# A spectral-plus-dense layer on one core: fewer opening fills on TensorE, and three GpSimd steps set further back

## The chip, the cores and the metric

The kernel runs on one core of a Trainium2 chip. TensorE (PE in the profile) does the matmuls, VectorE (DVE), ScalarE (ACT) and GpSimd (POOL) do the elementwise work, and SyncE (SP) issues the DMA transfers. The metric is device time in microseconds (us), the median over several runs.

## The reference, cut to what matters

Two stages over one tensor x of 2048 rows by 512 columns in bf16:

```python
h  = x + irfft2(rfft2(layernorm(x)) * (w_r + 1j * w_i))
h2 = h + relu(layernorm(h) @ w1 + b1) ** 2 @ w2 + b2
```

The layernorms run along the 512 columns. The kernel does the Fourier transforms as matmuls with tables of sines.

## The kernel before, in words

**Tiling.** The 2048 rows lie on 128 partitions, 16 rows ("groups", g = 0 to 15) on each, so a tile of one group is 128x512. The opening does three things at once: it loads x in six DMA pieces, it takes mean and variance of each group (`bn_stats` on DVE, line 385, with two groups on ACT, lines 376 and 379), and it builds the tables of sines from index tiles.

**Tables.** GpSimd writes index tiles with `iota` (line 293). DVE, ACT or GpSimd multiply them into phases (`fiE` at lines 340 and 342, `fiG` at line 332, `fiI` at line 461), and ACT takes the sine. `KF` (line 335, DVE) is a mask table: for each partition it keeps the values of `kft` where a comparison holds, zero elsewhere. `idxE` has 1152 elements a partition, and line 342 (GpSimd) is the wide operation on it; line 340 is its twin on ACT.

**First transform step.** For each group g, the mask table is scaled by the reciprocal deviation of the rows: `rs` is raised to the power -0.5 on GpSimd (line 392) in batches of 2, 4, 4, 3, 2 and 1 groups, and `KR[g] = KF * rs` (line 401: groups 0 to 8 on GpSimd, 10 to 15 on DVE; group 9 on ACT, line 398). Four matmuls a group (lines 408 and 409, function `s1`) then use `KR[g]`. Groups 0 to 9 go in five pairs into wide PSUM tiles (`m_p`, two buffers), each emptied into `Bt` by one ACT copy (line 424). Groups 10 to 15 go in units into narrow PSUM tiles (`s_p`, four buffers), emptied by ACT and DVE in turn (line 440). The next step (line 505) reads all of `Bt`, and after it a chain of DVE, ACT and PE work runs through the spectrum to about 48 us, followed by the two dense matmuls (lines 905 and 934) to the end.

**Fills.** At the very start TensorE has nothing to do. `fill` (line 356) issues matmuls of a zero tile `fz` against itself, 128x512 each, so that TensorE is running when the first real matmul comes. There are eight such calls, planned 0.9 us apart. Besides, every new PSUM tile calls `warm` (line 234), which adds small 128x128 matmuls of zeros where the plan sees a gap of over 0.3 us on TensorE:

```python
for _ in range(min(20, int(plan.gap * 0.6 / 0.0625)) if plan.gap > 0.3 else 0):
    mm(p[:, 0:P], lhsT=fz[:, 0:P], rhs=fz[:, 0:P], start=True, stop=True)
```

**What sets the order.** All steps are handed to a planner (class `Plan`) with an engine, an estimated duration, what they read and write, a priority (lower goes first) and an optional `order` (start after the named step). It plays the program through once with these estimates and issues the instructions in the order found; the order on each engine is then fixed by `pin`. What the planner takes as `reads` or `order` only shapes this order. The waits that the chip makes come from the data that an instruction really touches. So a step that is listed as reading `KF`, but does not touch it, gets a place in the queue from that and no wait.

**Other names.** `ident` is the 128x128 identity (lines 311 and 312), read by TensorE first at line 471 (at 28.9 us) and then for residuals and transposes. `idxD` is the index tile that `fiI` (line 461) is made from; `GI`, its sine, is taken on ACT at 34.5 us. `pF[:, 5:7]` (line 459, DVE copy of two integers a partition, from the `iota` of line 309) is the multiplier for `fiI`.

Of the kernel before, what the change touches and what calls it, by code (L numbers as in the profile page):

```python
# [9 lines left out]
ALU = mybir.AluOpType  # L10
# [5 lines left out]
P = 128  # L16
QT = 16384
# [16 lines left out]
class Plan:  # L34
# [13 lines left out]
    def add(self, eng, w, fn, reads=(), writes=(), prio=0.0, alloc=None, at=0.0, shared=False, lag=0.0,  # L48
            uses=(), order=()):
        many = isinstance(eng, tuple)  # L50
        ways = dict(zip(eng, w)) if many else {eng: w}
        t = dict(many=many, eng=None, ways=ways, w=0.0, fn=fn, reads=list(reads), writes=list(writes), prio=prio, alloc=alloc, at=at,
                 shared=shared, lag=lag, end=None, order=list(order), n=len(self.tasks))
        self.tasks.append(t)
        for k in t["writes"]:
            self.made.setdefault(k, []).append(t)
        for k in set(t["reads"]) | set(t["writes"]) | set(uses):
            self.use.setdefault(k, []).append(t)
# [82 lines left out]
def kernel(  # L141
# [17 lines left out]
    G = 16  # L159
# [16 lines left out]
    ident = persist.tile([P, P], BF16, name="ident")  # L176
# [19 lines left out]
    KF = fwd.tile([P, 2, P], BF16, name="KF")  # L196
    KR = fwd.tile([P, G, 2, P], BF16, name="KR")
# [10 lines left out]
    pI = tab.tile([P, 8], I32, name="pI")  # L208
    pF = tab.tile([P, 8], FP32, name="pF")
    cE = tab.tile([P, 1], FP32, name="cE")  # L210
# [4 lines left out]
    idxE = tab.tile([P, 9 * P], I32, name="idxE")  # L215
# [3 lines left out]
    fiE = [tab.tile([P, 9 * P], I32, name=f"fiE{i}") for i in range(2)]  # L219
    fiI = tab.tile([P, 4, 256], I32, name="fiI")  # L220
    idxD = tab.tile([P, 256], I32, name="idxD")
# [4 lines left out]
    gp, ve, sc, pe, sy = nc.gpsimd, nc.vector, nc.scalar, nc.tensor, nc.sync  # L226
# [5 lines left out]
    add = plan.add  # L232
# [31 lines left out]
    for c, (a, b) in enumerate(CH):  # L264
        add("SP", 0.45, lambda a=a, b=b: sy.dma_start(xs[:, a:b, :], xv[:, a:b, :]),
            writes=[("x", g) for g in range(a, b)], prio=c, at=0.7, lag=LAND[c])
# [4 lines left out]
    for i in range(2):  # L271
        add("SP", 2.0, lambda i=i: sy.dma_start(wx[i][:].rearrange("k j l -> j k l"),
                                                wv[i].rearrange("k j l -> j k l")[9:16, ::-1, 1:L + 1]),
            writes=[("wx", i)], prio=6 + i, at=1.0, lag=5.0)
    for i in range(2):
        add("SP", 1.0, lambda i=i: (sy.dma_start(W[:, i], wv[i][:, 0:8, 1:L + 1]),
                                        sy.dma_start(W[:, 2 + i, 0], wv[i][:, 8, 1:L + 1])), writes=[("Wn", i)],
            prio=8 + i, at=1.0, lag=6.0)
    for i in range(2):
        add("SP", 1.0, lambda i=i: sy.dma_start(W[:, 2 + i, 1:8], wx[i][:, ::-1]), reads=[("wx", i)], writes=[("Wr", i)],  # L280
            prio=10 + i, lag=6.0)

    def pool(w, fn, prio, reads=(), writes=()):
        add("POOL", w, fn, reads=reads, writes=writes, prio=prio)

    def dve(w, fn, prio, reads=(), writes=(), shared=False, **k):
        add("DVE", w, fn, reads=reads, writes=writes, prio=prio, shared=shared, **k)
# [4 lines left out]
    def iota(dst, pattern, base, cm):  # L292
        gp.iota(dst, pattern=pattern, base=base, channel_multiplier=cm)
# [4 lines left out]
         writes=["idxE"])  # L298
    pool(0.14, lambda: iota(pI[:, 3:5], [[16384, 2]], 0, 128), 0.15, writes=["p1"])
    pool(0.2, lambda: iota(rowq[:].rearrange("p h (k u) -> p h k u", u=2), [[0, 2], [4096, 8], [0, 2]], 0, 0), 0.4,  # L300
         writes=["rowq0"])
    pool(0.1, lambda: gp.memset(rowq[:, :, 1:2], 8 * 4096), 0.5, reads=["rowq0"], writes=["rowq"])
    pool(0.2, lambda: iota(offq[:].rearrange("p h (k u) -> p h k u", u=2), [[-HT, 2], [0, 8], [-QT, 2]], QT, 0), 0.6,
         writes=["offq0"])
# [3 lines left out]
         writes=["idxG"])  # L308
    pool(0.14, lambda: iota(pI[:, 5:7], [[128, 2]], 128, 256), 1.0, writes=["p2"])
    pool(0.1, lambda: gp.memset(mhalf[:], -0.5), 0.85, writes=["mhalf"])  # L310
    pool(0.1, lambda: gp.memset(ident[:], 0.0), 1.2, writes=["id0"])
    pool(0.3, lambda: gp.affine_select(out=ident[:], in_=ident[:], compare_op=ALU.not_equal, fill=1.0, base=0,
                                       pattern=[[-1, P]], channel_multiplier=1), 1.3, reads=["id0"], writes=["ident"])
    pool(0.34, lambda: iota(idxD[:], [[1, 256]], 0, 0), 1.4, writes=["idxD"])

    dve(0.15, lambda: ve.memset(mv1[:], 0.0), 0.06, writes=["mv1z"])
    dve(0.15, lambda: ve.memset(qtc[:], float(QT)), 0.0, writes=["qtc"])
# [3 lines left out]
        reads=["p0"], writes=["p01"])  # L321
    dve(0.15, lambda: ve.tensor_single_scalar(pI[:, 2:3], pI[:, 0:1], 7, ALU.bitwise_and), 0.2,
        reads=["p0"], writes=["p02"])
    dve(0.15, lambda: ve.scalar_tensor_tensor(cE[:], pI[:, 1:2], -4064.0, pI[:, 7:8], ALU.mult, ALU.add), 0.3,
        reads=["p01", "p7"], writes=["cE"], shared=True)
    dve(0.17, lambda: ve.tensor_copy(pF[:, 0:5], pI[:, 0:5]), 0.4, reads=["p01", "p02", "p1"], writes=["pF"],
        shared=True)
    dve(0.2, lambda: ve.scalar_tensor_tensor(flat(fiK), flat(rowq[:]), pF[:, 1:2], flat(offq[:]), ALU.mult, ALU.add),
        0.4, reads=["pF", "rowq", "offq"], writes=["fiK"], shared=True)
    for t in range(2):  # L330
        for r in range(2):
            add(("DVE", "POOL")[t], (0.36, 0.46)[t], lambda t=t, r=r: (ve, gp)[t].tensor_scalar(
                fiG[:, t, r, :], idxG[:], pF[:, 3 + t:4 + t], float((QT, HT)[r]), ALU.mult, ALU.add),
                prio=(0.45, 0.92)[t], reads=["pF", "idxG"], writes=[("fiG", t)])
# [4 lines left out]
    dve(0.3, lambda: ve.memset(fz[:], 0.0), 0.05, writes=["fz"])  # L339
    act(1.26, lambda: sc.activation(fiE[0][:], idxE[:], ACT.Identity, scale=cE[:]), 0.3, reads=["idxE", "cE"],  # L340
        writes=["fiE0"])
    pool(1.4, lambda: gp.tensor_scalar(fiE[1][:], idxE[:], cE[:], float(QT), ALU.mult, ALU.add), 0.95,
         reads=["idxE", "cE"], writes=["fiE1"])
    act(0.2, lambda: sin_of(flat(kft[:]), lo(fiK[:])), -50.0, reads=["fiK"], writes=["kft"])
    for t in range(2):
        act(0.62, lambda t=t: sin_of(flat(GF[:, t]), lo(flat(fiG[:, t]))), 0.6 + t / 10, reads=[("fiG", t)],
            writes=[("gf", t)])
    dve(0.15, lambda: ve.tensor_scalar(GF[:, :, :, 255:256], GF[:, :, :, 255:256], 0.5, None, ALU.mult), 54.0, reads=[("gf", 0), ("gf", 1)],
        order=[("KR", G - 1)], writes=["GF"])
    for i in range(2):  # L350
        act(1.16, lambda i=i: sin_of(flat(EF[:, i]), lo(fiE[i][:])), 0.5 + i / 10, reads=[f"fiE{i}"],
            writes=[f"EF{i}"])
    dve(0.46, lambda: ve.tensor_scalar(EF[:, 2], EF[:, 0], -1.0, None, ALU.mult), 78.0, reads=["EF0"],
        order=["BtD"], writes=["EF2"])

    def fill(key, n, prio, reads=(), at=0.0):
        def go():
            p = sg_tile(key)
            for _ in range(n):
                mm(p[:, 0:512], lhsT=fz[:, 0:P], rhs=fz[:], start=True, stop=True)  # L360
        add("PE", n * 0.216, go, reads=["fz", *reads], writes=[key], prio=prio, alloc=("sg", key), at=at)

    for i in range(8):
        fill(("fa", i), 4 if i < 6 else 3, -1.0, at=1.3 + 0.9 * i)

    ON_ACT = (3, 6)
    SQ = 5
# [4 lines left out]
    for bi, (a, b) in enumerate(BATCH):  # L372
        z = 10 * min(bi, 4) + 10
        for g in range(a, b):
            if g in ON_ACT:
                act(0.76, lambda g=g: sc.activation(junk[:], xs[:, g, :], ACT.Identity, scale=-RT / D,
                                                    accum_out=nmr[:, g:g + 1]), z - 30, reads=[("x", g)],
                    writes=[("sm", g)])
                act(0.82, lambda g=g: sc.activation(junk[:], xs[:, g, :], ACT.Square, scale=RT, bias=nmr[:, g:g + 1],
                                                    accum_out=mv1[:, g, 1:2]), z - 30, reads=[("x", g), ("sm", g), "mv1z"],  # L380
                    writes=[("mv", g)])
            else:
                def bn(g=g):
# [4 lines left out]
                    writes=[("mv", g)])  # L388
        mvs = [("mv", g) for g in range(a, b)]
        dve(0.13, lambda a=a, b=b: ve.tensor_scalar(rs1[:, a:b], mv1[:, a:b, 1], EPS, float(WSC ** -2), ALU.add, ALU.mult), z - 1,  # L390
            reads=mvs, writes=[("va", bi)])
        pool(0.42 + 0.155 * (b - a), lambda a=a, b=b: gp.tensor_tensor(rs1[:, a:b], rs1[:, a:b], mhalf[:, 0:b - a],
                                                                     ALU.pow), z - 1, reads=[("va", bi), "mhalf"],
             writes=[("rs", bi)])
        for g in range(a, b):
            e = "POOL" if g in KRP else "DVE"
            if g in KRA:
                act(0.4, lambda g=g: sc.activation(flat(KR[:, g]), flat(KF[:]), ACT.Identity, scale=rs1[:, g:g + 1]), z - 5,
                    reads=[("rs", bi), "KF"], writes=[("KR", g)])
# [3 lines left out]
                reads=[("rs", bi), "KF"], writes=[("KR", g)], shared=e == "DVE")  # L403
# [7 lines left out]
    for g in range(BIG):  # L411
        key = ("p1", g // 2)

        def big(g=g, key=key):
# [5 lines left out]
            writes=[key] + [("p1a", g // 2)] * (1 - g % 2), prio=10 + g, alloc=None if g % 2 else ("mm", key))  # L420
# [6 lines left out]
    for a, b in UNITS:  # L427
        n = b - a
        for t in range(2):
            k, eng = ("p1", a, t), ("ACT", "DVE")[t]  # L430
            for g in range(a, b):
                def half(a=a, g=g, t=t, k=k):
# [3 lines left out]
                    writes=[("p1a", a, t)] * (g == a) + [k] * (g == b - 1), prio=10 + a + t / 4, alloc=("sg", k) if g == a else None)  # L436

            def e2(a=a, b=b, t=t, k=k, eng=eng):
# [3 lines left out]
                writes=["Bt"] + ["BtD"] * (t == 1 and b == G), prio=56 + a)  # L442
# [6 lines left out]
    for k, (d, s) in ((0, (W1[:], B_w1.rearrange("(c p) f -> p c f", p=P))),  # L449
# [3 lines left out]
            order=[("EI", i) for i in range(4)] + [("Wr", 0), ("Wr", 1), ("Wn", 0), ("Wn", 1)])  # L453
# [2 lines left out]
    BY_PE = tuple(range(PE0, PE1, PES))  # L456
    dve(0.25, lambda: ve.tensor_scalar(CN[:, 0:len(BY_PE)], EF[:, 1, PE0:PE1:PES], -1.0, None, ALU.mult), 75.0, reads=["EF1"],
        order=["EF2"], writes=["CN"])
    dve(0.13, lambda: ve.tensor_copy(pF[:, 5:7], pI[:, 5:7]), 0.65, reads=["p2"], writes=["pF2"], shared=True)
    for lt in range(4):  # L460
        pool(0.48, lambda lt=lt: gp.tensor_scalar(fiI[:, lt], idxD[:], pF[:, 5 + lt % 2:6 + lt % 2],
                                                  float((QT, HT)[lt // 2]), ALU.mult, ALU.add), 400.0,
             reads=["pF2", "idxD", ("KR", G - 1)], writes=["fiI"])
    dve(0.15, lambda: ve.tensor_scalar(nm1[:], mv1[:, :, 0], -1.0, None, ALU.mult), 190.0,
        reads=[("mv", g) for g in range(G)], order=["EF2"], writes=["nm0"])
    dve(0.15, lambda: ve.tensor_scalar(nm1[:, 3:7:3], nmr[:, 3:7:3], 1.0 / RT, None, ALU.mult), 190.0,
        reads=["nm0"], writes=["nm1"], shared=True)
# [18 lines left out]
    for pr, first in ((0, 1), (1, 1), *((p, 0) for p in range(8))):  # L486
# [12 lines left out]
        if first or pr > 1:  # L499
# [7 lines left out]
            for q in range(2):  # L507
                add("PE", 0.46, lambda pr=pr, q=q, s2=s2: s2(pr, q), reads=["Bt", "GF"],
                    order=[("p2", pr, j) for j in range(q)], writes=[("p2", pr), ("p2", pr, q)], prio=z + 2 if pr > 1 else 80.2 + pr / 10,
# [7 lines left out]
            if pr == 0:  # L517
                for q in range(2):
                    eng = ("ACT", "DVE")[q]
                    add(eng, (0.6, 0.67)[q], lambda pr=pr, eu=eu, q=q, eng=eng: eu(pr, q, q + 1, COPY[eng], q == 0),  # L520
                        reads=[("p2", pr, q)], order=[("U", pr, 0)] * q, writes=[("U", pr), ("U", pr, q)],
                        alloc=None if q else ("U", ("U", pr)), prio=z + 2)
            elif pr == 1:
                for q in range(2):
                    add(("ACT", "DVE"), (0.6, 0.67), lambda e, pr=pr, eu=eu, q=q: eu(pr, q, q + 1, COPY[e], q == 0),
                        reads=[("p2", pr, q)], order=[("U", pr, 0)] * q, writes=[("U", pr), ("U", pr, q)],
# [5 lines left out]
        if pr == 0 and first:  # L532
# [11 lines left out]
            for u in range(2):  # L544
                add("PE", 0.46, lambda u=u, s3z=s3z: s3z(u), reads=[("U", 0, u), "EF0", "EF1", "EF2"], order=[("p3", 0, j) for j in range(u)],
                    writes=[("p3", 0, u)], prio=z + 1, alloc=("sg", ("p3", 0, u)))
                add(("ACT", "DVE")[u], (0.59, 0.66)[u], lambda u=u, ea0=ea0: ea0(u), prio=z + 1, reads=[("p3", 0, u)],
                    order=[("X", 0, 0)] * u, writes=[("X", 0), ("Xu", u)] + [("X", 0, 0)] * (1 - u),
                    alloc=None if u else ("AB", ("X", 0)))
        elif pr > 0 and not first:  # L550
            def s3(pr=pr):
# [25 lines left out]
                reads=[("U", pr), "EF0", "EF1", "EF2"] + (["CN"] if pr in BY_PE else []), writes=[("p3", pr)],  # L577
                prio=z + 1, alloc=("mm", ("p3", pr)))
# [5 lines left out]
            if ab[0] == "AB":  # L584
# [6 lines left out]
                for h in range(2):  # L591
                    dve(0.34, lambda pr=pr, h=h: bf(pr, h), z, reads=[("AB", pr)],
                        order=[("Xh", pr)] * h,
                        writes=[("X", pr)] + [("Xh", pr)] * (1 - h), alloc=("X", ("X", pr)) if h == 0 else None)
# [9 lines left out]
        for u in range(2) if pr == 0 else ():  # L604
            dve(0.61, lambda u=u, prod=prod: prod(0, u, 1), z, reads=[("Xu", u), ("Wn", 0), ("Wn", 1)], uses=[("X", 0)],
                order=["mh"] * u, writes=[("m", 0)] + ["mh"] * (1 - u), alloc=None if u else ("m", ("m", 0)))
        if pr:
            dve(1.14, prod, z, reads=[("X", pr), ("Wn", 0), ("Wn", 1), ("Wr", 0), ("Wr", 1)],
                writes=[("m", pr)], alloc=("m", ("m", pr)))
# [4 lines left out]
        for r in range(2):  # L614
            dve(0.34, lambda pr=pr, r=r: zz(pr, r), z, reads=[("m", pr)],
                order=[("Zh", pr)] * r,
                writes=[("Z", pr)] + [("Zh", pr)] * (1 - r), alloc=("Z", ("Z", pr)) if r == 0 else None)
        if pr > 0:
# [8 lines left out]
            for h in range(2):  # L627
                dve(0.34, lambda pr=pr, h=h: fold(pr, h), z, reads=[("Z", pr)],
                        order=[("Mh", pr)] * h,
                    writes=[("M", pr)] + [("Mh", pr)] * (1 - h), alloc=("M", ("M", pr)) if h == 0 else None)  # L630
# [20 lines left out]
        for h in range(2):  # L651
            add("PE", 0.46, lambda pr=pr, h=h, s4=s4: s4(pr, h),
                reads=[("M" if pr else "Z", pr), ("EI", 0), ("EI", 1), ("EI", 2)], order=[("p4", pr, 0)] * h,
                writes=[("p4", pr), ("p4", pr, h)], prio=z + 32 * (pr < 5),
# [8 lines left out]
        else:  # L663
            for h in range(2):
                eng = ("ACT", "DVE")[h]
                add(eng, (0.24, 0.22)[h], lambda et=et, h=h, eng=eng: et(COPY[eng], 7, 0, 2, 2 * h, 2 * h + 2), prio=z,
                    reads=[("p4", 7, h)], writes=["T2a"])
                add(eng, (0.52, 0.6)[h], lambda et=et, h=h, eng=eng: et(COPY[eng], 7, 2, G, 2 * h, 2 * h + 2), prio=z + 90,
                    reads=[("p4", 7, h)], order=["T2a"], writes=["T2"])
# [33 lines left out]
    for g in range(2):  # L703
        for e in (1, 0):
            ptag = "ph" if (g, e) == (1, 0) else "pp"

            def d5(g=g, e=e, ptag=ptag):
# [4 lines left out]
                prio=z - 1, alloc=(ptag, ("pd", g, e)))  # L712

            def deo(eng, g=g, e=e):
                COPY[eng](EO[:, g, 1 - e], T["pd", g, e][:, 0:256])
            add(("ACT", "DVE"), (0.37, 0.36), deo, reads=[("pd", g, e)], order=[("EO", g, 1)] * (1 - e),
                writes=[("EO", g, e)], prio=z + g)
# [9 lines left out]
    for c, (a, b) in enumerate(CHUNKS):  # L727
# [3 lines left out]
        for g in range(a, b):  # L731
            z = late + g
            if c > 0:
# [18 lines left out]
                for i in range(2):  # L752
                    dve(0.36, lambda g=g, i=i: lv1(g, i), z, reads=[("p5", g), ("od", g)],
                        order=[("qh", g)] * i + [("un", 1)] * (c == 1),
                        writes=[("q", g), ("qh", g)] if i == 0 else [("q", g)], alloc=("qb" if g in BY_PE2 else "q", ("q", g)) if i == 0 else None)
# [16 lines left out]
                else:  # L772
# [16 lines left out]
                    reads=[("p6", g)], writes=[("hs", g)])  # L789
                act(0.91, lambda g=g: sq_of(hs[:, g, :], g), z, reads=[("hs", g)], writes=[("ss", g)])  # L790
            if c:
                add(("DVE", "POOL")[HBP], (0.62, 1.3)[HBP], lambda g=g: (ve, gp)[HBP].tensor_tensor(hb[:, g, :], hs[:, g, :], b2b[:], ALU.add),  # L792
                    prio=late + 180 + g, reads=[("hs", g), ("FW", 3)], order=[("ph", c, 4)], writes=[("hb", g)])

        if c == 0:
            for g in range(2):
# [9 lines left out]
                for k in range(3):  # L806
                    add("PE", 0.22, lambda g=g, k=k, d6=d6: d6(g, k),
                        reads=[["ident"], [("EO", g, 1), ("EI", 3)], [("EO", g, 0)]][k],
# [5 lines left out]
                else:  # L814
# [5 lines left out]
                    writes=[("sd", 0, g)])  # L820
                dve(0.16, lambda g=g: ve.reciprocal(rs2[:, g:g + 1], rs2[:, g:g + 1]), -30.0, reads=[("sd", 0, g)],
                    writes=[("r2", 0, g)])
# [156 lines left out]
```

## Time and profile before

| what | value |
|---|---|
| median of 4 runs | 161.84 us (161.82 to 162.92) |
| the profiled execution's own time | 162.92 us |
| its span, first to last instruction | 161.1 us |
| PE busy | 154.3 us (96%) |
| DVE busy | 121.7 us (76%) |
| ACT busy | 101.7 us (63%) |
| POOL busy | 33.3 us (21%) |
| opening fills on PE, line 360 | 30 matmuls, 9.0 us |
| first real matmul, line 408 | starts at 10.83 us |

The profiled execution is the slowest of the four runs, 1.1 us over the other three, which lie within 0.04 us of each other. The page gives busy times, the span in 40 slices, the chain of work that ended last (followed back from the end), and groups of instructions. A row of the timeline is: start, length, engine, line, operation, what it writes and reads, and how many instructions were merged; the bracket at its end tells idle time before it and what ended that. PEld is TensorE's loading of weights, which runs beside the matmuls.

### The profile page before, as it was taken

What the parts mean: (1) busy time and instruction counts of PE and PEld (TensorE: products, weight loads), DVE (VectorE), ACT (ScalarE), POOL (GpSimd) and SP (SyncE); (2) the same over time, 40 slices, a digit from 0 to 9 for tenths busy, and PEclk for the clock granted to TensorE, in tenths of its full rate; (3) what the DMA queues carried; (4) which work ended last, traced back from release to release, by engine and by line L of the source; (5) the groups of instructions that cost most, each with busy time, mean ns of one, the idle gap of its engine ahead of it and who ended that gap; (6) DMA issues with size and microseconds to landing.
All of it is one profiled execution on the core that took longest, in us unless ns stands there. A gap on an engine that the chain in (4) does not pass through costs nothing.

```text
span 161.1 us, 2895 instructions
## 1 busy us (share of the span) xinstructions
PE 154.3 (96%) x1025; PEld 92.3 (57%) x1034; DVE 121.7 (76%) x325; ACT 101.7 (63%) x186; POOL 33.3 (21%) x83
## 2 busy tenths in 40 slices
PE   6999999999989899999999999999999999999992
PEld 3358866677668687465644544444544444465461
DVE  6999789999977996879882799993398971385321
ACT  8947968999886798479730789730389830188100
POOL 8789600000000015022240003351002240000000
PEclk9999999999999999999999999999999999999999
DMA  4956989994000001010313000115100122010011
GB/s 155 287 187 182 262 204 218 395 365 131 2 4 0 0 4 35 27 40 4 65 33 98 33 0 4 33 37 128 65 2 4 34 64 65 33 35 4 0 65 33
DMA packets 21017, 13.43 MB, mean 83 GB/s; under 512 B 9738, under 2 KB 19722, under 8 KB 21002
## 3 DMA queue, kind: packets, MB, share of 16 engines
q1 hardware_dynamic: 21002, 13.25, 30.1%
q8 instruction: 8, 0.13, 0.3%
q14 instruction: 7, 0.06, 0.1%
HBM read 8.92 MB, written 3.01 MB: 74 GB/s over the span
## 4 chain that ended last, share of the span: by engine, by line
PE 90%; DVE 5%; ACT 2%; issue 1%; DVEq 0%
PE po L934 30%; PE sg L905 20%; PE ph L905 10%; PE s_fa L360 5%; PE m_p L484 5%; PE m_p L505 4%; PE m_p L650 2%; PE pp L760 1%; PE m_p L236 1%; PE pp L767 1%; PE m_p L408 1%; PE m_p L409 1%; PE s_p L408 1%; DVE Z L613 1%; PE s_p L409 1%
## 5 line engine op out<-in xcount | busy, mean ns | idle before, releaser
L934 PE MATMUL po<-W,act 128*128 128x512 bf16 (+1 forms) x229 | 48.7, 366 | 0.5
L917 ACT ACTIVATE rl<-sg,b1f 128x384 bf16<-128x384 f32 (+2 forms) x46 | 27.3, 602 | 21.9 <-PE sg L905 20.6
L905 PEld LDWEIGHTS <-W 128*128 128x128 bf16 x288 | 26.8, 98 | 19.6 <-issue 0.2
L905 PE MATMUL sg<-UT,W 128*128 128x384 bf16 (+2 forms) x184 | 37.2, 337 | 0.0
L934 PEld LDWEIGHTS <-act 128*128 128x128 bf16 x238 | 23.2, 98 | 24.1
L923 DVE TENSOR_TENSOR act<-rl 128x384 bf16<-128x384 bf16 (+2 forms) x70 | 25.0, 367 | 6.5 <-ACT rl L917 6.1
L943 DVE TENSOR_TENSOR ot<-po,hb 128x512 bf16<-128x512 f32 (+1 forms) x17 | 11.2, 659 | 20.7 <-PE po L934 20.5
L852 POOL TENSOR_SCALAR rs<-ss 128x1 f32<-128x1 f32 x14 | 6.1, 437 | 93.4 <-ACT junk L672 93.4
L917 ACT ACTIVATE rl<-ph,b1f 128x512 bf16<-128x512 f32 (+2 forms) x23 | 13.9, 602 | 10.0 <-PE ph L905 9.4
L905 PE MATMUL ph<-UT,W 128*128 128x512 bf16 (+3 forms) x96 | 19.9, 330 | 0.1
L788 DVE TENSOR_TENSOR hs<-pp,xs 128x512 bf16<-128x512 f32 x14 | 9.7, 689 | 2.3 <-PE pp L760 1.3
L672 ACT ACTIVATE junk<-hs,nm 128x512 bf16<-128x512 bf16 x14 | 10.0, 714 | 0.1
L484 PE MATMUL m_p<-U,EF 128*128 128x512 bf16 (+1 forms) x46 | 9.5, 337 | 0.0
L783 DVE TENSOR_TENSOR R<-q 128x127 bf16<-128x127 f32 x40 | 9.4, 284 | 0.0
L385 DVE BATCH_NORM_STATS2 st<-xs 128x6 f32<-128x512 bf16 x14 | 9.0, 670 | 0.3 <-DMA xs<-in_A_x_dram 0.3
L792 DVE TENSOR_TENSOR hb<-hs,b2b 128x512 f32<-128x512 bf16 x14 | 9.1, 682 | 0.0
L360 PE MATMUL s_fa<-fz 128*128 128x512 bf16 x30 | 9.0, 475 | 0.0
L854 POOL TENSOR_TENSOR rs<-rs,mhalf 128x1 f32<-128x1 f32 x14 | 7.9, 568 | 1.2
L582 ACT CAST AB<-m_p 128x1024 bf16<-128x1024 f32 x7 | 7.1, 1018 | 1.6 <-PE m_p L484 1.6
L750 DVE TENSOR_TENSOR q<-pp,od 128x256 f32<-128x256 f32 x20 | 7.6, 415 | 0.0
L505 PEld LDWEIGHTS <-Bt 128*128 128x128 bf16 x64 | 6.1, 97 | 1.9 <-issue 0.6
L505 PE MATMUL m_p<-GF,Bt 128*128 128x256 bf16 x56 | 6.8, 272 | 0.2 <-ACT AB L543 0.2
(159 smaller groups left out, 225.6 us busy)
## 6 DMA issues: line engine op xcount, KB each, us to landing
W<-in_B_w_dram SPq DMA_DIRECT2D x2, 1792.0 KB, 10.3
out_dram<-ot SPq DMA_DIRECT2D x15, 128.0 KB, 1.8
xs<-in_A_x_dram SPq DMA_DIRECT2D x4, 256.0 KB, 3.8
xs<-in_A_x_dram SPq DMA_DIRECT2D x2, 512.0 KB, 7.3
W<-wx SPq DMA_DIRECT2D x2, 448.0 KB
W<-in_A_w_r_dram SPq DMA_DIRECT2D x1, 512.0 KB, 7.7
W<-in_A_w_i_dram SPq DMA_DIRECT2D x1, 512.0 KB, 6.2
wx<-in_A_w_r_dram SPq DMA_DIRECT2D x1, 448.0 KB
```

The costliest lines, as they stand in the source:

```text
L360: mm(p[:, 0:512], lhsT=fz[:, 0:P], rhs=fz[:], start=True, stop=True)
L484: mm(o.rearrange("p (j i e) -> p j i e", e=2, i=RUN), lhsT=w, rhs=U[:, q, s].rearrange("p (j e i) -> p j i e", e=2, i=RUN), **k)
L505: mm(puv[:, e, :], lhsT=Bt[:, 2 * t + 1 - e, 2 * pr + q, :], rhs=gfv[:, t, :, e, :], start=(t == 0), stop=(t == 1))
L672: sc.activation(junk[:], src, ACT.Square, bias=nm1[:, g:g + 1], accum_out=ss2[:, g:g + 1])
L783: ve.tensor_tensor(o, x, y, (ALU.add, ALU.subtract, ALU.subtract, ALU.add)[k])
L788: dve(0.66, lambda g=g: ve.tensor_tensor(hs[:, g, :], T["p6", g][:], xs[:, g, :], ALU.add), z, reads=[("p6", g)], writes=[("hs", g)])
L792: add(("DVE", "POOL")[HBP], (0.62, 1.3)[HBP], lambda g=g: (ve, gp)[HBP].tensor_tensor(hb[:, g, :], hs[:, g, :], b2b[:], ALU.add), prio=lat ...
L905: mm(p[:, P * i0:P * i1], lhsT=W1[:, d, bass.ts(f, P)], rhs=T["UT", c][:, i0:i1, d, :], start=(d == 0), stop=(d == ND - 1))
L917: sc.activation(r[:, 0:P * n], T["ph", c, f][:, 0:P * n], ACT.Relu, bias=b1f[:, f:f + 1], scale=1.0)
L923: ve.tensor_tensor(t[:, f, 0:P * n], r[:, 0:P * n], r[:, 0:P * n], ALU.mult)
L934: mm(p[:, cs], lhsT=T["act", c][:, f, bass.ts(i, P)], rhs=W2[:, f, cs], start=(f == 0), stop=(f == NF - 1))
L943: ve.tensor_tensor(o[:, cs], T["po", g, h][:, cs], hb[:, g, cs], ALU.add)
```

## The change

The fills go from six calls of 4 and two of 3 to four of 3 and four of 2. On GpSimd, the three steps that make `ident` and `idxD` get a late priority and an `order` behind `KR[15]`. The wide operation of line 342 gets a later priority and is listed as reading `KF`. The small copy of line 459 on DVE gets a slightly later priority.

```diff
-    def pool(w, fn, prio, reads=(), writes=()):
-        add("POOL", w, fn, reads=reads, writes=writes, prio=prio)
+    def pool(w, fn, prio, reads=(), writes=(), **k):
+        add("POOL", w, fn, reads=reads, writes=writes, prio=prio, **k)
...
-    pool(0.1, lambda: gp.memset(ident[:], 0.0), 1.2, writes=["id0"])
+    pool(0.1, lambda: gp.memset(ident[:], 0.0), 390.0, writes=["id0"], order=[("KR", G - 1)])
     pool(0.3, lambda: gp.affine_select(out=ident[:], in_=ident[:], compare_op=ALU.not_equal, fill=1.0, base=0,
-                                       pattern=[[-1, P]], channel_multiplier=1), 1.3, reads=["id0"], writes=["ident"])
-    pool(0.34, lambda: iota(idxD[:], [[1, 256]], 0, 0), 1.4, writes=["idxD"])
+                                       pattern=[[-1, P]], channel_multiplier=1), 390.0, reads=["id0"], writes=["ident"])
+    pool(0.34, lambda: iota(idxD[:], [[1, 256]], 0, 0), 395.0, writes=["idxD"], order=[("KR", G - 1)])
...
-    pool(1.4, lambda: gp.tensor_scalar(fiE[1][:], idxE[:], cE[:], float(QT), ALU.mult, ALU.add), 0.95,
-         reads=["idxE", "cE"], writes=["fiE1"])
+    pool(1.4, lambda: gp.tensor_scalar(fiE[1][:], idxE[:], cE[:], float(QT), ALU.mult, ALU.add), 1.5,
+         reads=["idxE", "cE", "KF"], writes=["fiE1"])
...
     for i in range(8):
-        fill(("fa", i), 4 if i < 6 else 3, -1.0, at=1.3 + 0.9 * i)
+        fill(("fa", i), 3 if i < 4 else 2, -1.0, at=1.3 + 0.9 * i)
...
-    dve(0.13, lambda: ve.tensor_copy(pF[:, 5:7], pI[:, 5:7]), 0.65, reads=["p2"], writes=["pF2"], shared=True)
+    dve(0.13, lambda: ve.tensor_copy(pF[:, 5:7], pI[:, 5:7]), 0.75, reads=["p2"], writes=["pF2"], shared=True)
```

In the order that the planner makes of it:

- **TensorE** has 20 fills instead of 30, four small `warm` matmuls ahead of each of the last three fill calls (12), and three ahead of the first real matmul, where there were none. The `warm` matmuls further on are as many as before (15, 9 and 4). In the narrow units, the second half of groups 12 and 13 keeps its place, and only buffer names differ.
- **GpSimd** runs the `iota` of line 309 ahead of line 342 instead of behind it, and the three steps for `ident` and `idxD` after the last power of line 392, ahead of `fiI`. Line 342 itself still follows `fiG` with only that short `iota` between, and has no wait on `KF`.
- **DVE** runs the copy of line 459 directly behind `KF` instead of two `bn_stats` later.
- **ACT** swaps two sines: the second half of `GF` comes ahead of the second `EF` table.
- **SP** is unchanged.

## The prediction

> **What bounds the kernel now.** I read the page first (busy times, slices, chain), then the chain of waits for the first 24 us, then each engine's timeline there.
>
> ```profile
> PE 154.3 (96%) x1025; PEld 92.3 (57%) x1034; DVE 121.7 (76%) x325; ACT 101.7 (63%) x186; POOL 33.3 (21%) x83
> ...
> PEclk9999999999999999999999999999999999999999
> ...
> PE 90%; DVE 5%; ACT 2%; issue 1%; DVEq 0%
> ...
> L360 PE MATMUL s_fa<-fz 128*128 128x512 bf16 x30 | 9.0, 475 | 0.0
> ```
>
> PE fills the chain, but 9 us of that are fills that compute nothing. In the opening the question is therefore what PE would otherwise wait for. The chain of waits there:
>
> ```profile
> 2.16 8.84 PE s_fa L360 x30
> 11.00 0.11 PE m_p L408
> ...
> 11.87 0.84 PE m_p L236 x15
> ...
> 13.62 1.02 ACT Bt L424
> 14.64 0.04 issue
> 14.68 0.66 PE m_p L236 x9
> ...
> 20.12 0.39 PE s_p L236 x7
> ```
>
> The chain runs through all 30 fills into the first real matmul, then through PE's own queue. It touches GpSimd nowhere. Yet GpSimd's timeline shows the operands ready early at first:
>
> ```profile
> 4.29 1.23 POOL L342 TENSOR_SCALAR fiE<-idxE,cE 128x1152 int32<-128x1152 int32 x1
> 5.47 0.13 POOL L293 IOTA pI<- 128x2 int32 x1
> ...
> 7.49 0.73 POOL L392 TENSOR_TENSOR rs<-rs,mhalf 128x2 f32<-128x2 f32 x1 [1.05 <-DVE rs L390]
> 8.32 0.94 POOL L401 TENSOR_SCALAR KR<-KF,rs 128x256 bf16<-128x256 bf16 x2
> 9.54 1.03 POOL L392 TENSOR_TENSOR rs<-rs,mhalf 128x4 f32<-128x4 f32 x1 [0.28 <-DVE rs L390]
> 10.66 1.85 POOL L401 TENSOR_SCALAR KR<-KF,rs 128x256 bf16<-128x256 bf16 x4
> ```
>
> KR[0] is there at 8.80 and KR[1] at 9.26, but PE takes them up at 10.83, when the fills are done. So up to 1.5 us of the fills is delay. From 9.54 on GpSimd has no idle time until 18.85: powers and KR[2] to KR[8] follow each other (KR[3] at 11.60, KR[5] at 12.51, KR[7] at 14.55, KR[8] at 15.01, the next power at 15.83, which DVE's KR[10] at 15.86 waits for). That is the second floor, only just below PE.
>
> **The change part by part.**
>
> *Fills.* The weight loads show how long each fill takes:
>
> ```profile
> 5.79 0.15 PEld L360 LDWEIGHTS <-fz 128*128 128x128 bf16 x1 [0.28 <-issue]
> 6.22 0.15 PEld L360 LDWEIGHTS <-fz 128*128 128x128 bf16 x1 [0.28 <-issue]
> 6.65 3.85 PEld L360 LDWEIGHTS <-fz 128*128 128x128 bf16 x18 [0.28 <-issue]
> ```
>
> Up to about 6.7 us they come 0.427 us apart, afterwards 3.85/18 = 0.214. So about 11.4 fills run at half rate (1.95 + 11.4 x 0.427 + 18.6 x 0.216 = 10.83, the observed start of the real work), though the PEclk row says full clock all along. The ten fills dropped are ten fast ones: 10 x 0.216 = 2.16 us. The 15 added small matmuls cost 0.0556 each (15 of them took 0.84): 0.83. PE is free at 10.83 - 1.33 = 9.51, after KR[1].
>
> *GpSimd's three moved steps* (0.20 + 0.29 + 0.34 = 0.83 us at 5.55 to 6.43) lay in a hole: the power at 7.49 waited 1.05 us for DVE. Taking them out brings nothing there. Behind the last power (17.13) they delay `fiI` from 18.85 to about 19.7, and `GI` reads it on ACT at 34.5; `ident` is first read at 28.9 and would exist at 17.6. Cost nil, with 11 us of cover. The collision to check is DVE's eviction at line 440 beside GpSimd: 691 ns with GpSimd busy (18.22) and 692 without (19.10), so none.
>
> *Line 342, line 335 and line 459.* Here two rows speak:
>
> ```profile
> 1.47 0.78 DVE L326 CAST pF<-pI 128x5 f32<-128x5 int32 x1
> ...
> 4.36 1.42 DVE L335 SCALAR_TENSOR_TENSOR KF<-sub,pF,kft 128x256 bf16<-128x256 int32 x1
> ```
>
> KF, 256 elements, takes 1.42 us and ends 0.27 after GpSimd's 1152-element operation; the cast, 5 elements, takes 0.78 and ends 0.03 after GpSimd's 1152-element iota. Both sat behind GpSimd. [...]
> - GpSimd first: KF ends 0.08 later, and the cast behind it, now ahead of the first `bn_aggr`, costs 0.06 which it no longer costs later. DVE's statistics end 0.07 later.
> - KF first: KF ends near 4.75, but the cast behind it then sits behind line 342, which ends near 5.95, as line 326 did. Statistics end about 0.11 later.
> - KF and the cast both first: statistics start 0.9 earlier, but groups 8 and 9 land at 9.48 and DVE took group 8 at 9.52 already, so only KR[0] to KR[8] gain (about 0.7).
>
> I take 0.09 (between the first two), with -0.7 and +0.11 as ends. ACT's swapped sines end where they did (9.69), and SP reads `EF` first at 17.07.
>
> *The new course*, with 0.09 on every GpSimd time, 0.05 from an engine's end to PE's start (as ACT 14.63 to PE 14.68), 0.31 from a pair's last matmul to its eviction (11.60 to 11.91), 0.109 a matmul:
> - Pair 0: PE 9.51 to 10.39, evicted 10.58 to 11.59. The 15 small matmuls end at 11.22.
> - Pair 1: second half waits for KR[3], 11.74; evicted 12.38 to 13.39 (before: 13.62).
> - Pair 2: second half waits for KR[5], 12.65; evicted 13.29 to 14.30.
> - Pair 3: its buffer is free at 13.44, nine small matmuls to 13.94, then KR[7], 14.69; evicted 15.33.
> - Pair 4: KR[8], 15.15; evicted 16.24 to 17.26 (before: 17.16 to 18.18).
> - Units: PE starts with KR[10] at 16.29 and runs to 18.15, waiting for evictions after; ACT's third eviction ends at 18.83, which frees the last buffer; DVE's last eviction is 19.30 to 19.72 (before: 20.15 to 20.58).
>
> So 10 us of fills are exchanged for GpSimd's floor, and the 1.33 us on PE shrink to 20.58 - 19.72 = 0.86 at the last eviction. That is what line 505 waits for (its second matmul starts at 20.635), and from there all is a shift: DVE's spectrum chain starts 0.86 earlier. What it could run into: W's first half landed at 21.74 and is read at 23.96; EI[0] landed at 22.72 and ACT reads it at 23.40, which would be 22.54, a delay of 0.2 into a 0.48 us hole; the weights for the dense part landed at 33.2 and 39.0, and are read at 53.9 and 60.7. All hold. From 54 us on PE is the chain.
>
> *Sum.* The profiled execution is 162.92 = 161.1 span + 1.8 around it; it would be 162.06, with a span of 160.2. The other runs stand 1.1 us lower; on the median the same 0.86 gives **161.0 us**.
>
> [...] The row says 11.4 slow fills, rate restored at 6.7. [...]
>
> **Rivals.**
> - *Fills as profiled, floor by GpSimd* (above): 161.0.
> - *The fills were not on the path in the unprofiled runs* (rate restored early): no gain, DVE's 0.07 to 0.11 remain: 161.9. For it: the 1.1 us. Against: the narrow scatter.
> [...]
> [...]
>
> **How the numbers follow.** Chances: first case 0.50, hidden fills 0.32, KF first 0.10, clock 0.08. A measurement here tells about 0.5% from no change, which is 0.81 us, so 161.03 is the border. The first case sits on it: 0.86 plus or minus 0.25 puts somewhat over half, say 0.28 of its 0.50, on the faster side, with 0.10 of KF first: 0.38 in all. Slower by over 0.5% is the clock case, less the part of it that stays small, plus a little for hidden fills with a larger DVE delay: 0.08. Within: 0.54. The first case's own range is 160.7 to 161.3. The full one reaches to hidden fills above with DVE's delay and below into KF first: 160.5 to 162.1.
>
> **What would show it.** First real matmul at about 9.5; KR[3] on GpSimd at about 11.7, with PE waiting for POOL ahead of pairs 1, 2 and 3; the last eviction of line 440 at about 19.7; KF still near 1.4 us with line 342 beside it, or about 0.4 with the cast near 1.2 in its place; `fiI` ending near 19.7; everything after 22 us shifted alike. The forecast fails if fills end before 9 us in the timed runs, if a weight transfer or EI holds up DVE after 22 us, or if matmuls after 9.5 come 0.2 us apart.

## The result, and the profile after

The changed kernel takes 161.55 us in the median of 43 runs (160.91 to 162.05), the kernel before 162.23 in the median of 64 (161.52 to 163.12). The ratio is 0.9957, with a 95% interval of 0.9946 to 0.9968: 0.43% faster, 0.7 us. The profiled executions stand at 162.05 against 162.92, and their spans at 160.3 against 161.1.

The median of the kernel before was 161.84 in the four runs that the forecast had. Over 64 runs it is 162.23, because the runs spread over 1.6 us. That spread turned out to be part of the answer.

The page after (busy times, clock row, chain), with the group of fills:

```profile
PE 152.7 (95%) x1030; PEld 92.0 (57%) x1039; DVE 121.5 (76%) x325; ACT 101.8 (63%) x186; POOL 33.4 (21%) x83
...
PEclk9999999999999999999999999999999999999999
...
PE 83%; DVE 7%; POOL 3%; DMA 2%; issue 2%; ACT 2%; DVEq 0%
...
L360 PE MATMUL s_fa<-fz 128*128 128x512 bf16 x20 | 6.5, 470 | 0.0
```

PE's share of the chain falls from 90% to 83%; DVE, GpSimd and a DMA come in. The chain of waits of the first 24 us shows where:

```profile
0.72 3.17 DMA xs<-in_A_x_dram
...
4.52 1.36 DVE KF L335
...
9.63 1.03 POOL rs L392
10.66 0.09 issue
10.75 1.85 POOL KR L401 x4
12.60 0.98 POOL rs L392
13.58 0.09 issue
13.67 0.51 POOL KR L401
14.17 0.04 issue
14.22 0.27 PE m_p L408
...
19.23 0.39 PE s_p L236 x7
```

No fill is on it. It runs from the first piece of x through the mask table, DVE's statistics and GpSimd's powers and tables, and reaches PE at 14.22. Its last row here, the small matmuls ahead of line 505, ends at 19.62, where before it ended at 20.51.

GpSimd's and TensorE's timelines after:

```profile
4.38 1.23 POOL L342 TENSOR_SCALAR fiE<-idxE,cE 128x1152 int32<-128x1152 int32 x1
7.65 0.73 POOL L392 TENSOR_TENSOR rs<-rs,mhalf 128x2 f32<-128x2 f32 x1 [2.04 <-DVE rs L390]
8.47 0.94 POOL L401 TENSOR_SCALAR KR<-KF,rs 128x256 bf16<-128x256 bf16 x2
```

```profile
9.01 0.27 PE L408 MATMUL m_p<-KR,xs 128*128 128x256 bf16 x1 [0.23 <-POOL KR L401]
...
11.28 0.27 PE L408 MATMUL m_p<-KR,xs 128*128 128x256 bf16 x1 [0.39 <-POOL KR L401]
```

The hole ahead of the first power grew from 1.05 to 2.04 us, so the three steps taken out of it (0.83 us) were indeed hidden. PE now waits for GpSimd ahead of pairs 0 and 1. The last eviction of line 440 ends at 19.69 us, 0.89 earlier than before.

The fills reach full rate at another moment than before. The weight loads come close together from 4.94 us on, not from 6.65:

```profile
4.51 0.15 PEld L360 LDWEIGHTS <-fz 128*128 128x128 bf16 x1 [0.28 <-issue]
4.94 1.22 PEld L360 LDWEIGHTS <-fz 128*128 128x128 bf16 x6 [0.28 <-issue]
```

The fill that starts at 4.94 is followed by the next after 0.25 us, between the 0.427 of the slow fills and the 0.216 of the fast ones, so the rate changed within it, at about 5.0 (an estimate from these three spacings). In the profile before, the same working gives 6.8. This is called the moment of full rate below.

### The profile page after: what moved, and what is told of

Its sections match the earlier page's. It is cut to its first block, busy times and chain, and to the rows that moved or that the text cites. A ratio compares the mean times of both kernels' runs of the same rounds, so it can differ in the third digit from the quotient of the medians.

```text
span 160.3 us, 2907 instructions
## 1 busy us (share of the span) xinstructions
PE 152.7 (95%) x1030; PEld 92.0 (57%) x1039; DVE 121.5 (76%) x325; ACT 101.8 (63%) x186; POOL 33.4 (21%) x83
## 4 chain that ended last, share of the span: by engine, by line
PE 83%; DVE 7%; POOL 3%; DMA 2%; issue 2%; ACT 2%; DVEq 0%
PE po L934 30%; PE sg L905 20%; PE ph L905 10%; PE m_p L484 5%; PE m_p L505 4%; DMA xs<-in_A_x_dram 2%; PE m_p L650 2%; DVE st L385 2%; POOL KR L401 1%; PE pp L760 1%; POOL rs L392 1%; PE pp L767 1%; PE s_p L408 1%; DVE Z L613 1%; DVE KF L335 1%
## 5 line engine op out<-in xcount | busy, mean ns | idle before, releaser
L905 PEld LDWEIGHTS <-W 128*128 128x128 bf16 x288 | 26.8, 98 | 19.7 <-issue 0.2
L236 PEld LDWEIGHTS <-fz 128*128 128x128 bf16 x78 | 5.5, 101 | 3.1 <-DVE pI L320 1.2
```

Of the source, the lines that this page charges most:

```text
L905: mm(p[:, P * i0:P * i1], lhsT=W1[:, d, bass.ts(f, P)], rhs=T["UT", c][:, i0:i1, d, :], start=(d == 0), stop=(d == ND - 1))
```

## The experiments

In the listings of kernels with an added line, line numbers stand one to three higher than in the kernel before.

### The two halves alone

The fills alone:

```diff
-        fill(("fa", i), 4 if i < 6 else 3, -1.0, at=1.3 + 0.9 * i)
+        fill(("fa", i), 3 if i < 4 else 2, -1.0, at=1.3 + 0.9 * i)
```

> The fills alone: 20 instead of 30 on TensorE, everything on GpSimd, DVE and ACT in the order of the kernel before. Theory of the forecast (fills delay TensorE, GpSimd's chain of powers and scaled tables is the next floor, the moved GpSimd steps bring nothing): the whole gain is here, ratio 0.995 to 0.996, first real matmul near 9.0 to 9.5 us, last eviction of line 440 near 19.6. Rival (the GpSimd steps carry the gain): ratio within 0.001 of 1. In both the median may lie up to 0.1 us below that of the whole change, since the short copy of line 459 stays where it was.

Measured: 161.95 us (160.97 to 162.29, 22 runs), ratio 0.9968 (0.9952 to 0.9983). First real matmul at 9.30, last eviction at 19.60. Of the 22 runs, 17 lie between 161.85 and 162.06.

The other half, with 30 fills:

```diff
-        fill(("fa", i), 3 if i < 4 else 2, -1.0, at=1.3 + 0.9 * i)
+        fill(("fa", i), 4 if i < 6 else 3, -1.0, at=1.3 + 0.9 * i)
```

(against the changed kernel)

> The other half alone: 30 fills, but line 342, ident, idxD and the copy of line 459 placed as in the change. Theory of the forecast: nothing, ratio 0.999 to 1.001, since the three steps lay in a hole of GpSimd that waited 1.05 us for DVE, and TensorE comes late anyway. Rival (the steps carry the gain): ratio 0.996.

Measured: 162.28 us (161.94 to 163.02, 14 runs), ratio 0.9997 (0.9978 to 1.0016). The GpSimd half alone shows no effect, and the fills alone bring 0.32% of the 0.43%. The intervals don't separate 0.9968 from 0.9957. The GpSimd half stands behind 30 fills here, so this run can't tell what it does behind 20. How the runs are spread differs: with the fills alone 4 of 22 runs lie below 161.85, in the changed kernel 26 of its 43. These are two sets of measurements, though; measured in one set with the fills alone, the changed kernel has 4 of 16 (next experiment). The next experiments ask what makes these faster runs.

### The changed kernel once more

> The changed kernel once more, for a second profile. Its 43 runs lie between 160.91 and 162.05 us, 17 of them within 0.13 us of the upper end. If the spread is the moment at which TensorE reaches full rate, a profile with a late moment is slower than one with an early one. [...]

Measured: 161.94 us in the median of 16 runs (161.0 to 162.03), ratio 0.9957 (0.9939 to 0.9976). The profiled execution took 161.0, one of the shortest, and 1.05 us less than the first profile of the same kernel. DVE's and GpSimd's timelines in it:

```profile
3.70 0.69 DVE L385 BATCH_NORM_STATS2 st<-xs 128x6 f32<-128x512 bf16 x1 [0.22 <-DMA xs<-in_A_x_dram]
4.31 0.47 DVE L335 SCALAR_TENSOR_TENSOR KF<-sub,pF,kft 128x256 bf16<-128x256 int32 x1
4.70 0.16 DVE L459 CAST pF<-pI 128x2 f32<-128x2 int32 x1
```

```profile
4.37 1.50 POOL L342 TENSOR_SCALAR fiE<-idxE,cE 128x1152 int32<-128x1152 int32 x1
6.55 0.73 POOL L392 TENSOR_TENSOR rs<-rs,mhalf 128x2 f32<-128x2 f32 x1 [0.68 <-DVE rs L390]
```

Here KF started 0.06 ahead of line 342, took 0.47 us instead of 1.36, and GpSimd's operation was the one that took longer (1.50 instead of 1.23). The first power starts at 6.55, 1.1 us earlier than at 7.65. The moment of full rate was 5.2 us in this run and 5.0 in the slower one, so that is not what tells the two apart.

The profile of the second half alone shows a third order:

```profile
4.38 0.47 DVE L335 SCALAR_TENSOR_TENSOR KF<-sub,pF,kft 128x256 bf16<-128x256 int32 x1
4.77 1.12 DVE L459 CAST pF<-pI 128x2 f32<-128x2 int32 x1
5.79 0.17 DVE L387 BATCH_NORM_AGGREGATE mv<-st 128x2 f32<-128x6 f32 x1
```

KF was quick, but the copy of two integers behind it took 1.12 us and ended with GpSimd's operation (4.37 to 5.86). The statistics then came no earlier than with KF held up.

As these three profiles have it, what decides is when KF asks. It does so when the first `bn_stats` ends, and that waits for the first piece of x: it started at 3.70 in the run with both quick, 3.77 with KF quick alone, 3.91 with KF held up.

### Taking the collision away, or forcing its order

The wide index operation on ACT (its constant `QT` as a bias tile that the kernel already has):

```diff
-    pool(1.4, lambda: gp.tensor_scalar(fiE[1][:], idxE[:], cE[:], float(QT), ALU.mult, ALU.add), 1.5,
-         reads=["idxE", "cE", "KF"], writes=["fiE1"])
+    act(1.26, lambda: sc.activation(fiE[1][:], idxE[:], ACT.Identity, scale=cE[:], bias=qtc[:]), 0.55,
+        reads=["idxE", "cE", "qtc"], writes=["fiE1"])
```

> The change, but the wide index operation of line 342 is done on ACT instead of GpSimd, so that nothing of GpSimd stands beside the mask table of line 335. Theory that GpSimd's operation holds up the mask table: KF takes 0.4 us instead of 1.36 to 1.42, the statistics of the first groups are 0.8 us earlier, KR[8] about 0.7 earlier, and the run is 0.3 to 0.5 us faster than the change (ratio to before near 0.993), in nearly every run. If KF's 1.4 us is its own: KF stays at 1.4 and the ratio stays at 0.9957.

Measured: 161.43 us, six runs from 161.42 to 161.45, ratio 0.9937 (0.9912 to 0.9961). In its profile DVE shows

```profile
4.40 0.47 DVE L335 SCALAR_TENSOR_TENSOR KF<-sub,pF,kft 128x256 bf16<-128x256 int32 x1
4.79 0.16 DVE L459 CAST pF<-pI 128x2 f32<-128x2 int32 x1
```

with KF as quick although x came at 3.79. So the 1.4 us were the wait for GpSimd. The six runs agree within 0.03 us. They do not reach 161.0. ACT's queue is fuller: its first emptying of a pair starts at 10.81, where the 161.0 run had 9.80. That this is the reason was not tested.

The other direction, DVE's short copy directly ahead of KF, so that KF asks later, and mostly behind line 342:

```diff
-    dve(0.13, lambda: ve.tensor_copy(pF[:, 5:7], pI[:, 5:7]), 0.75, reads=["p2"], writes=["pF2"], shared=True)
+    dve(0.13, lambda: ve.tensor_copy(pF[:, 5:7], pI[:, 5:7]), 0.65, reads=["p2"], writes=["pF2"], shared=True)
```

> [...] Theory (the order of these requests decides): KF ends after line 342, near 5.9, and nearly every run lies at 162.0 to 162.2, none or one below 161.8. If the spread of the change comes from elsewhere: about half the runs between 160.9 and 161.8, as in the change.

Measured: 162.00 us (161.95 to 162.53, 11 runs, none below 161.85), ratio 0.9969 (0.9955 to 0.9982). KF asked later and was held:

```profile
4.43 0.15 DVE L459 CAST pF<-pI 128x2 f32<-128x2 int32 x1
4.50 1.37 DVE L335 SCALAR_TENSOR_TENSOR KF<-sub,pF,kft 128x256 bf16<-128x256 int32 x1
```

That no run is below 161.85 supports the order as the cause, but weakly: in this set the kernel before has no run below 162.14 either, where it went down to 161.93 and less in the other sets, and the changed kernel was not measured in it. One run, at 162.53, lies above the expected range; the profile is of a run at 162.0 and does not show it.

Now the order that the change's `reads` names but does not bring about: GpSimd copies one element of KF first, and so waits for it.

```diff
+    pool(0.1, lambda: gp.tensor_copy(kfs[:], KF[:, 0, 0:1]), 1.45, reads=["KF"], writes=["kfs"])
     pool(1.4, lambda: gp.tensor_scalar(fiE[1][:], idxE[:], cE[:], float(QT), ALU.mult, ALU.add), 1.5,
-         reads=["idxE", "cE", "KF"], writes=["fiE1"])
+         reads=["idxE", "cE", "kfs"], writes=["fiE1"])
```

> The change plus one GpSimd copy of a single KF element ahead of line 342, so that the wide index operation really waits for the mask table. [...] If the spread of the change has another cause (the moment of full rate alone), the runs at 162.0 stay.

Measured: 161.36 us (161.15 to 161.73, 12 runs), ratio 0.9943 (0.9922 to 0.9964). No run lies at 162.0. KF is quick although x came at 3.87:

```profile
4.48 0.47 DVE L336 SCALAR_TENSOR_TENSOR KF<-sub,pF,kft 128x256 bf16<-128x256 int32 x1
4.86 0.16 DVE L461 CAST pF<-pI 128x2 f32<-128x2 int32 x1
```

With GpSimd early, its chain of waits starts with fills again:

```profile
2.16 5.31 PE s_fa L362 x14
7.47 0.22 PE s_fa L237 x4
7.69 0.43 PE s_fa L362 x2
```

And the same with 30 fills:

```diff
-        fill(("fa", i), 3 if i < 4 else 2, -1.0, at=1.3 + 0.9 * i)
+        fill(("fa", i), 4 if i < 6 else 3, -1.0, at=1.3 + 0.9 * i)
```

> As mask_first_20_fills, but with the 30 fills of the kernel before. Theory (an earlier mask table is hidden while TensorE is still in its fills): close to the kernel before, ratio 0.996 to 1.000, with runs from about 161.5 to 163.1 and the runs just below 162.0 gone to lower times. If the mask table carries the gain by itself: ratio 0.994 as with 20 fills.

Measured: 162.47 us (161.55 to 163.07, 20 runs), ratio 1.0003 (0.9983 to 1.0022). Behind 30 fills the early mask table is worth nothing in the median, as expected: there are two floors, the fills and GpSimd's chain, and the later one counts.

### How few fills

From mask_first_20_fills, with no small matmuls between the fills:

```diff
-            p = sg_tile(key)
+            p = T[key] = psg.tile([P, 512], FP32, tag="sg", name="s_" + str(key[0]), bufs=nps[1])
...
-        fill(("fa", i), 3 if i < 4 else 2, -1.0, at=1.3 + 0.9 * i)
+        fill(("fa", i), 2 if i < 4 else 1, -1.0, at=1.3 + 0.9 * i)
```

> As mask_first_20_fills, with 12 fills and no small matmuls between them. Theory (floor by GpSimd once fills are out of the way): the fills end at 7.1 to 7.7 us, ahead of KR[0], TensorE idles up to 0.8 us, and every run lies at about 160.9 to 161.1, ratio 0.992. Rival (the clock falls back or is released later when TensorE is not filled up to its first real matmul): a part of the runs is 1 us or more slower than 161.5, with matmuls 0.2 us apart after 9 us.

Measured: 161.32 us (160.95 to 161.95, 11 runs), ratio 0.9931 (0.9907 to 0.9956). Every run was expected at 160.9 to 161.1; three of the 11 are there (160.95, 160.96, 161.0). The profile is of the longest, at 161.95; PE's timeline and the clock row of its page:

```profile
5.52 0.44 PE L237 MATMUL m_p<-fz 128*128 128x128 bf16 x5
8.00 0.31 PE L410 MATMUL m_p<-KR,xs 128*128 128x256 bf16 x1 [2.03 <-POOL KR L403]
...
8.74 0.42 PE L410 MATMUL m_p<-KR,xs 128*128 128x256 bf16 x1
8.95 0.42 PE L411 MATMUL m_p<-KR,xs 128*128 128x256 bf16 x1
...
11.68 0.27 PE L411 MATMUL m_p<-KR,xs 128*128 128x256 bf16 x1
11.79 0.27 PE L410 MATMUL m_p<-KR,xs 128*128 128x256 bf16 x1
```

```profile
PEclk9959999999999999999999999999999999999999
```

Here the clock fell back, to 0.50. Full rate came early, the fills were over by 5.96, PE idled 2.03 us, and from about 8.1 to 11.5 the matmuls start 0.213 us apart instead of 0.109. Shares by stretch (busy time, then the granted clock after it):

```profile
4.70:8.10 3.40, 1.37 (x11) 0.77 (x10) 3.40 (x13) 3.37 (x10) 2.76 (x5) 1.00 0.98 333
8.10:11.50 3.40, 3.40 (x25) 2.90 (x24) 3.06 (x11) 2.58 (x4) 3.09 (x6) 0.50 0.55 172
```

PE was busy for 1.37 of the 3.4 us ahead, and was granted 0.50 for the next 3.4. That the idling brought the half rate is inferred from this order; no run shows what the clock goes by.

This explains one run only. The mean granted clock is 0.989 for it and 0.998 to 1.000 for the other ten, which spread from 160.95 to 161.59 all the same; what spreads those is open. Nor is it all of the 0.8 us by which this profile is longer than the next one (161.15): the last eviction ends 0.59 later (19.38 against 18.79), and then DVE waits 0.3 us for the second part of `W`, which can be read only at 25.9. So in this profile the load of `W` is a further floor, just behind the opening.

With 16 fills (`2` in all eight calls):

```diff
-        fill(("fa", i), 2 if i < 4 else 1, -1.0, at=1.3 + 0.9 * i)
+        fill(("fa", i), 2, -1.0, at=1.3 + 0.9 * i)
```

> As mask_first_12_fills with 16 fills, no small matmuls between them. The fills then end between about 6.7 us (full rate early) and 8.5 us (full rate late), against KR[0] at about 7.95. Theory (12 fills were slow where TensorE then idled over 2 of 3.4 us and fell back to half rate): at most 1.3 us of idling, no fall back, no run above 161.5, median about 161.1, ratio 0.993. If any idling ahead of the first real matmul brings the half rate back: runs up to 162 as with 12 fills.

Measured: 161.33 us (161.05 to 161.91, 11 runs), ratio 0.9949 (0.9929 to 0.9969). The median is 0.2 above what was expected, and three of the 11 runs are above 161.5, where none was expected. In its profile (161.15) PE idles 1.68 us, is busy for 1.97 of the 3.41 us behind the moment of full rate (4.45), and stays at full rate (mean granted clock 1.000). The three longer runs have a mean granted clock of 0.998 to 1.000, so they did not fall back as the 12 fills did (0.989); what held them up is open.

With no fills at all:

```diff
-    for i in range(8):
+    for i in range(0):
```

(against mask_first_20_fills)

> As mask_first_20_fills, with no fills at all; TensorE starts with 20 small matmuls that the planner puts ahead of the first real one. [...]

Measured: 162.08 us (161.21 to 162.58, 20 runs), ratio 0.9971 (0.9954 to 0.9988). PE is at half rate until 12.5 us there (matmuls 0.213 apart from 8.2 to 12.4), and yet its median is only 0.8 us above that with 12 fills. The half rate costs little because PE would otherwise wait for GpSimd: it reaches the second pair at 11.31, only 0.95 later than the profile with 16 fills, which waited for its table until 10.36.

Last, 16 fills without the 15 small matmuls ahead of the second pair:

```diff
-        warm(T[key])
+        if key != ("p1", 1):
+            warm(T[key])
```

(in `mm_tile`, against mask_first_16_fills)

> As mask_first_16_fills, without the 15 small matmuls (0.84 us) that the planner puts ahead of the second pair. If TensorE sets the pace there (it reaches the second pair at 11.15 in mask_first_20_fills while KR[3] is there at 10.75): up to 0.4 us faster than mask_first_16_fills, median about 160.8. If GpSimd's chain does: the same time.

Measured: 161.95 us (160.97 to 162.68, 12 runs), ratio 0.9973 (0.9951 to 0.9995), slower in the median than with them, though the two intervals overlap. The waits of its profile name two for DMA transfers:

```profile
ACT EI L477 <- DMA EI<-EF: 0.8, 1, 0.8
...
DVE m L606 <- DMA W<-wx: 0.4, 1, 0.4
```

The one for `EI` is in no other profile here, the one for `W` in that of 12 fills too. EI landed at 22.71 there, against 21.16 with the 15 matmuls, though SP issued both at 15.7. The edit also changed the order in the narrow units. Which of these slows the median is open; the last eviction, at 19.01 against 18.79, shows that the opening itself was no faster.

## Why the prediction was right, and where it was not

**The fills' working held.** The profiled execution was forecast at 162.06 with a span of 160.2, and came at 162.05 and 160.3. That the numbers meet this closely is luck of the draw: the second profile of the same kernel stands at 161.0. But it is the course that was forecast, with KF held up, and its steps held one by one: pair 1 evicted from 12.37 (forecast 12.38), pair 3 from 15.30 (15.33), the last eviction from 19.27 to 19.69 (19.30 to 19.72). The first real matmul came at 9.01, not at 9.51, since full rate came at 5.0 instead of 6.8; pair 1 waits for `KR[3]` either way, so nothing followed from it. The 10 fills leave, GpSimd's chain becomes the floor, and everything after 22 us shifts alike: the first dense matmul of line 905 starts at 52.97 instead of 53.86.

**GpSimd's three moved steps cost and brought nothing**, as far as the runs show: the second half alone is at 0.9997 with 30 fills, and with 20 the place they left is idle time. `fiI` ended at 19.90 (forecast 19.7).

**The term of 0.09 for DVE** measured 0.09 (the second power's input at 9.39 instead of 9.30) with GpSimd first. The 0.08 in it is the place of one `iota` on GpSimd: line 342 starts at 4.38 instead of 4.29. With KF first and the copy held up it is 0.02 (9.32), not 0.11. With KF and the copy both first, where the forecast has 0.7, the second power starts 1.01 earlier than in the kernel before (8.53 instead of 9.54).

**What failed is taking the one profile, and three runs that agree within 0.04 us, for the course of all runs.** The agreement of three runs was chance: 64 runs scatter over 1.6 us (161.52 to 163.12). It is not the toss between KF and line 342 that scatters them: with 30 fills and KF forced to be first, 20 runs still spread over 1.5 us. In the nine profiles that open with the same small matmuls and fills, the moment of full rate lies at 4.9, 5.0, 5.2, 6.0, 6.3, 6.4, 6.7, 6.8 and 7.2 us, whatever was changed. So in these profiles it differs by 2.3 us from run to run behind the same opening, and the profile that the forecast started from has one of the late ones, 6.8. What sets it was not shown.

The runs without a profile seem to show this moment as well. In five of the nine profiles the granted clock drops to 0.50 behind the last matmul, and each time 153.6 us after the moment of full rate (160.4 after 6.8 in the kernel before, 158.8 after 5.2 in the run at 161.0): an early drop near the end goes with an early full rate. In four of the five it pulls the mean granted clock of the whole run below 1 (0.997 to 0.999); in the fifth it comes only 0.1 us before the end. In the first profile of the changed kernel, with full rate at 5.0, the clock stays at 1.00 to the end. With 30 fills this mean sorts the runs completely. In the 171 runs of the kernel before and of the two experiments with 30 fills, measured beside the other kernels, the 59 with 0.997 to 0.999 are all at 162.60 us or more, and the 112 with 1.000 all at 162.60 or less. With the fills cut to 20 and nothing else changed it sorts nothing: the runs that crowd at 161.93 to 162.02 have both. So with 30 fills the time goes with the drop, and by the five profiles with the moment of full rate; with 20 fills it hardly does.

The 0.86 us are right for an execution with the fills as late as in that profile, and nothing for one that already stands near 161.95. Subtracting them from the median of 161.84 counted them against runs that did not have them. The measured median, 161.55, therefore lies in the full range (160.5 to 162.1) but outside the first case's own (160.7 to 161.3). The rival of hidden fills, given 0.32, describes a part of the runs, and not a different kernel. Over the runs, the mean falls by 0.55 us with the fills alone (162.39 to 161.85).

**Which of KF, the copy and line 342 comes first did differ from run to run, but the odds were wrong.** "KF and the cast both first" had a chance of 0.10. In the changed kernel 26 of the first 43 runs lie below 161.85, and in the second set 4 of 16; the profiled one of these is that case, at 161.0. On the path this case gains more than was forecast, since its last eviction ends at 18.61, where the profile with KF held up has 19.69. DVE took group 8 at 8.75 there, which the forecast had landing at 9.48. The kernel with the order reversed has none of 11, the one with the order forced has 12 of 12. Only one run below 161.85 was profiled in the changed kernel, so that all of them are this case is likely, not shown. In the run at 161.0 line 342 started at 4.37, while KF ran (4.31 to 4.78), and the copy behind KF still got through in 0.16 us. What was missed is what decides the toss, as the three profiles have it: the landing of the first piece of x, some 0.2 us different from run to run (the first `bn_stats` at 3.70, 3.77 and 3.91).

So the change has one effect that is shown, fills that no longer come late. A second is only possible: the `iota` ahead of line 342 delays it by 0.09 us (4.29 to 4.38), which would let KF be first more often. It was listed as a cost. The mean of the changed kernel is 161.61 in its first set and that of the fills alone 161.85, but measured in one set they are 161.81 and 161.85, with 4 of 16 and 4 of 22 runs below 161.85. Whether the GpSimd half adds anything to the fills is open.

**The clock falling back**, given 0.08, did not happen in the changed kernel: the matmuls behind 9.01 us start about 0.11 apart, and the mean granted clock is 1.000 in its first profile. With 12 fills it did (0.50 from 8.1 to 11.5 us). Waits of at most 0.39 us ahead of the pairs, in the changed kernel, and a gap of 1.68 us, with 16 fills, came without it, the gap of 2.03 us with 12 fills came with it. No run shows a loss of 0.5% by it in the changed kernel, and how much idling it takes was not measured.

## What to carry to other kernels

Fills have to end when the first real operand comes (with the mask table first, 20 fills took 161.36 us and 30 took 162.47). How long they last hung here on a moment that differed from run to run behind the same opening (4.9 to 7.2 us in nine profiles): one profile shows one draw of it, so look at the spread of the runs before subtracting a saving from their median. A planner's dependency without a data dependency is a hope; where two engines meet within a tenth of a microsecond, an instruction that really waits (here a copy of one element, with none of 12 runs at 162.0) turns a toss into an order. The kernels with the lowest ratios (mask_first_12_fills 0.9931, index_on_act 0.9937, mask_first_20_fills 0.9943) have intervals that overlap that of the change. They differ in how steady they are: the first spreads over 1.0 us from run to run, the second, in six runs, over 0.03, and the third over 0.6.

## What the runs showed of the hardware that was not expected

- The granted clock row does not show the half rate at the start (full in every slice, while fills come 0.427 us apart), but does show it when it returns: 0.50 from 8.1 to 11.5 us with 12 fills.
- The drop of the granted clock behind the last matmul comes 153.6 us after the moment of full rate, in all five profiles with fills that have it. Without fills it comes 146.8 us after (full rate at 12.6, drop at 159.3), which is 6.8 less, twice the 3.4 us that the half rate lasted with 12 fills. Whether the two lengths have to do with each other was not shown.
- With 12 fills PE was busy for 1.37 of the 3.4 us from 4.70 on and ran at half rate behind them; with 16 fills it was busy for 1.97 of the 3.41 us from 4.45 on and stayed at full rate. One profile each; what lies between was not measured.
- Two requests within 0.15 us end in three ways: KF 0.06 ahead of line 342, both DVE operations pass (0.47 and 0.16 us); KF about 0.01 behind it, KF passes and the copy of two elements is held (1.12); KF 0.07 to 0.14 behind, KF is held (1.36 to 1.42). The first two ways were seen in one profile each, the third in four. GpSimd's operation is lengthened from 1.23 to about 1.50 in the first two.
